# A channel layer as seven block products in place of eight, with its input kept per chunk in a ring

## The chip, the cores and the metric

The kernel runs on one core of one Trainium2 chip. The metric is the device time in microseconds (us) of one execution. Times are medians of several executions, beside executions of the kernel before on the same chip. "Granted clock" is the share of TensorE's full clock that the profile records. SBUF and PSUM are the core's two on-chip memories: in this program the inputs, weights and hidden values lie in SBUF, and the matmuls write PSUM. A relu is a maximum with 0. The engines are TensorE (PE; PEld is its weight load), VectorE (DVE), ScalarE (ACT), GpSimd (POOL) and SyncE (SP, which issues DMAs).

## The reference

For each of 8 batches of 3008 tokens x 256 features, the reference takes the real part of a 2-D Fourier transform, mixes the tokens, and applies a two-layer channel network with a residual:

```
X = np.fft.fft(np.fft.fft(x, axis=1), axis=2).real
h = np.maximum(X.transpose(0, 2, 1) @ w_tok1, 0.0) @ w_tok2
u = X + h.transpose(0, 2, 1)
h2 = np.maximum(u @ w_ch1, 0.0) @ w_ch2     # w_ch1 256 x 1536, w_ch2 1536 x 256
return u + h2
```

The change concerns the last product, `max(...) @ w_ch2`: per batch 3008 tokens x 1536 hidden units x 256 features.

## The kernel before

Tokens go in 48 chunks of 512 (six a batch). Each chunk is worked off in four quarters ("subs"). A quarter holds a quarter of this chunk's first layer (`mm1`, 6 matmuls of 512 columns), a quarter of the previous chunk's second layer (`mm2`, 12 matmuls of 256 columns), and between them pieces of the next batch's front (transform and token mixing). GpSimd "folds" the input of the batch after that: sums and differences of mirrored tokens and features.

```python
def mm1(b, c, c1, cts):                       # first layer + relu
    ...
        if ct % 3 < 2:
            nc.scalar.activation(out=c1[:, ct, 0:n], in_=pc[:, 0:n], func=AFT.Relu)
        else:
            ts(c1[:, ct, 0:n], pc[:, 0:n], 0.0, AT.max)           # VectorE
def mm2(b, c, c1, ks, box):                   # second layer, 128 tokens
    ...
    for ct in range(NCT if n else 0):         # NCT = 12 blocks of 128 hidden units
        nc.tensor.matmul(po[0:n, o:o + D], lhsT=c1[:, ct, ks * P:ks * P + n],
                         rhs=wc2[:, ct, :], start=(ct == 0), stop=(ct == NCT - 1))
    ...                                       # residual: VectorE, reads PSUM
def fold(b, engs):                            # engs: GpSimd for b >= 1
    for s, (t0, t1) in enumerate(((13, 17), (9, 13), (5, 9), (1, 5))):
        eng.tensor_tensor(out=xd[:, t, :], in0=xp[:, t, :], in1=rv, op=AT.subtract)
        eng.tensor_tensor(out=xp[:, t, :], in0=xp[:, t, :], in1=rv, op=AT.add)
        ...                                   # the same over mirrored features -> eo
        yield
```

## Time and profile before

The first executions took 630.45 us (630.44 to 632.22).

| engine | busy us | share of the span |
|---|---|---|
| PE | 608.3 | 97% |
| VectorE | 353.8 | 56% |
| ScalarE | 318.6 | 51% |
| GpSimd | 244.5 | 39% |

The page of the kernel before: the busy row, and the chain that ended last (the work, followed back from the last instruction) by engine.

```profile
PE 608.3 (97%) x4810; PEld 420.9 (67%) x4810; DVE 353.8 (56%) x809; ACT 318.6 (51%) x682; POOL 244.5 (39%) x234
...
PE 95%; ACT 2%; DVE 1%; issue 0%; DVEq 0%; POOL 0%; POOLq 0%
```

The waits of PE in the kernel before (who waited for whom: us in total, times, longest). The first line is the start-up; after it PE hardly waits.

```profile
PE pt L255 <- ACT tp L239: 11.7, 1, 11.7
PE po L598 <- DVE osb L615: 1.3, 2, 0.6
```

The chain of the kernel before in order of time (start us, us, what). Twelve second-layer matmuls of 256 columns take 1.31 us; 24 token-layer matmuls of 127 and 130 columns, each with its own weights, take 1.36 us.

```profile
366.51 1.36 PE pt L478 x24
...
369.19 1.31 PE po L598 x12
```

One line of the fold in the kernel before, on GpSimd and (in the start-up) on VectorE: count, then duration min/median/max in ns. On GpSimd it is 3.1 times as long, and its 28 durations differ by 17 ns at most: nothing disturbs it.

```profile
L413 POOL TENSOR_TENSOR xd<-xp,xm x28: 2110/2118/2127, 39.0 to 436.0; 94x1024 f16<-94x1024 f16 x28
...
L413 DVE TENSOR_TENSOR xd<-xp,xm x4: 675/678/678, 11.6 to 18.6; 94x1024 f16<-94x1024 f16 x4
```

So PE is the bound, and its time is the sum of what it streams.

### The profile page before, as it was taken

The page shows a single profiled execution, that of the slowest core. Times are in us where ns is not written, and L with a number is a line of the kernel's source. Part 1 is how long each engine was busy: PE and PEld are TensorE (multiplying, and loading weights), DVE is VectorE, ACT ScalarE, POOL GpSimd, SP SyncE. Part 2 cuts the span into 40 slices and gives each one's busy share as a digit, 9 for nine tenths or more (in the row PEclk, how much of TensorE's full clock was granted, in tenths as well). Part 3 has the DMA queues.
Part 4 walks back from the last instruction along what each step waited for, and adds up shares of the span by engine and source line. Part 5 has one row for each costly group of instructions (what it writes and reads, how often), then busy time and mean ns, then how long its engine had stood idle before and what let it go on. Part 6 is the DMA issues. An engine that isn't in the chain of part 4 may idle for free.

```text
span 628.7 us, 11983 instructions
## 1 busy us (share of the span) xinstructions
PE 608.3 (97%) x4810; PEld 420.9 (67%) x4810; DVE 353.8 (56%) x809; ACT 318.6 (51%) x682; POOL 244.5 (39%) x234
## 2 busy tenths in 40 slices
PE   2899999999999999999999999999999999999996
PEld 1766677667666766667666676667766676666664
DVE  8865455665654556455664557545565456544442
ACT  8875554644436453464435554374534654334441
POOL 8559698595033940369130880059200000000000
PEclk9999999999999999999999999999999999999999
DMA  9993835636315274333924258143223422335232
GB/s 143 212 182 100 157 66 96 134 68 133 72 34 110 60 145 61 82 63 63 168 58 68 66 100 139 35 93 68 52 51 76 77 52 54 80 68 85 60 84 67
DMA packets 86583, 56.28 MB, mean 90 GB/s; under 512 B 54864, under 2 KB 83472, under 8 KB 85776
## 3 DMA queue, kind: packets, MB, share of 16 engines
q1 hardware_dynamic: 78048, 37.84, 30.7%
q0 software_dynamic: 8256, 17.49, 16.2%
q8 instruction: 37, 0.61, 0.4%
q14 instruction: 18, 0.15, 0.1%
q10 hardware_dynamic: 224, 0.20, 0.1%
HBM read 34.98 MB, written 24.64 MB: 95 GB/s over the span
## 4 chain that ended last, share of the span: by engine, by line
PE 95%; ACT 2%; DVE 1%; issue 0%; DVEq 0%; POOL 0%; POOLq 0%
PE po L598 39%; PE pc L577 39%; PE pu L544 7%; PE pt L478 3%; PE pz L435 2%; PE pw L462 1%; PE pw L463 1%; PE py L509 1%; PE pq L509 1%; PE filler L273 1%; ACT tt L280 0%; PE ph L383 0%; PE ph L385 0%; PE pz L451 0%; ACT vq L308 0%
## 5 line engine op out<-in xcount | busy, mean ns | idle before, releaser
L580 ACT ACTIVATE c<-pc 128x512 f16<-128x512 f32 (+1 forms) x384 | 204.7, 586 | 164.6 <-PE pc L577 130.1
L598 PE MATMUL po<-wc,c 128*128 128x256 f16 x2256 | 276.8, 273 | 1.3 <-DVE osb L615 1.3
L598 PEld LDWEIGHTS <-c 128*128 128x128 f16 x2256 | 217.3, 98 | 49.6 <-issue 3.6
L87 DVE TENSOR_SCALAR c<-pc 128x512 f16<-128x512 f32 (+1 forms) x192 | 130.4, 679 | 125.7 <-PE pc L577 114.1
L577 PE MATMUL pc<-ut,wc1p 128*128 128x512 f16 x576 | 140.0, 379 | 0.0
L577 PE MATMUL pc<-ut,wc1m 128*128 128x512 f16 (+1 forms) x576 | 134.9, 371 | 0.0
L615 DVE TENSOR_TENSOR osb<-po,rt 128x258 f32<-128x258 f32 (+4 forms) x246 | 75.2, 356 | 50.4 <-PE po L598 47.7
L577 PEld LDWEIGHTS <-wc1m 128*128 128x128 f16 x576 | 54.8, 98 | 53.8
L577 PEld LDWEIGHTS <-wc1p 128*128 128x128 f16 x576 | 52.7, 98 | 48.3 <-issue 1.2
L552 DVE TENSOR_TENSOR ut<-pu,yt 128x512 f16<-128x512 f32 (+1 forms) x96 | 64.2, 670 | 20.1 <-PE pu L544 20.1
L413 POOL TENSOR_TENSOR xd<-xp,xm 94x1024 f16<-94x1024 f16 x28 | 59.3, 2118 | 14.4 <-DMA xm<-in_x_dram,ix 14.4
L635 POOL COPY ch<-c 128x768 f16<-128x768 f16 x4 | 3.3, 822 | 150.9 <-DVE c L87 150.9
L414 POOL TENSOR_TENSOR xp<-xp,xm 94x1024 f16<-94x1024 f16 x28 | 59.3, 2118 | 2.2
L418 POOL TENSOR_TENSOR eo<-xp 94x512 f16<-94x512 f16 (+1 forms) x28 | 33.9, 1211 | 59.0 <-PE pz L451 57.8
L637 POOL COPY c<-ch 128x768 f16<-128x768 f16 x4 | 3.3, 822 | 125.3 <-PE po L598 125.3
L280 ACT ACTIVATE w<-pw 128x127 f16<-128x127 f32 x96 | 26.1, 279 | 49.9 <-PE pw L463 49.9
L280 ACT ACTIVATE z<-pz 128x480 f16<-128x480 f32 (+1 forms) x60 | 38.9, 664 | 24.1 <-PE pz L435 18.6
L544 PE MATMUL pu<-w2p,uu 128*128 128x512 f16 (+1 forms) x168 | 50.0, 380 | 0.0
L516 DVE TENSOR_TENSOR yt<-py,qs 128x512 f16<-128x512 f32 x48 | 30.9, 686 | 27.5 <-PE pc L577 17.8
L465 DVE SCALAR_TENSOR_TENSOR w<-alt,pw 128x131 f16<-128x131 f16 x96 | 33.1, 350 | 18.3 <-ACT w L280 18.3
L422 POOL TENSOR_TENSOR eo<-xd 94x508 f16<-94x508 f16 (+1 forms) x28 | 33.7, 1203 | 0.0
L512 ACT ACTIVATE qs<-pq 128x512 f32<-128x512 f32 x24 | 14.4, 600 | 25.8 <-PE pq L509 18.0
(149 smaller groups left out, 402.2 us busy)
## 6 DMA issues: line engine op xcount, KB each, us to landing
out_dram<-osb SPq DMA_DIRECT2D x83, 256.0 KB, 3.5
xp<-in_x_dram POOLq DMA_DIRECT2D x16, 272.0 KB, 5.5
out_dram<-osb SPq DMA_DIRECT2D x11, 192.0 KB, 3.2
xp<-in_x_dram POOLq DMA_DIRECT2D x16, 127.5 KB, 6.0
rt<-ut SPq DMA_TRANSPOSE x96, 3.5
w2s<-in_moe_w_tok_dram POOLq DMA_DIRECT2D x1, 1504.0 KB, 17.5
w1p<-in_moe_w_tok_dram POOLq DMA_DIRECT2D x2, 384.0 KB, 8.8
wc<-in_moe_w_ch_dram POOLq DMA_DIRECT2D x1, 768.0 KB, 14.9
```

Of the source, the lines that this page charges most:

```text
L87: eng.tensor_scalar(out=out_, in0=in_, scalar1=s1, scalar2=None, op0=op0)
L280: nc.scalar.activation(out=out_, in_=in_, func=AFT.Copy)
L413: eng.tensor_tensor(out=xd[:, t, :], in0=xp[:, t, :], in1=rv, op=AT.subtract)
L414: eng.tensor_tensor(out=xp[:, t, :], in0=xp[:, t, :], in1=rv, op=AT.add)
L418: eng.tensor_tensor(out=eo[:, t, 1:129], in0=xp[:, t, 1:129], in1=xp[:, t, 255:127:-1], op=AT.add)
L422: eng.tensor_tensor(out=eo[:, t, 129:256], in0=xd[:, t, 1:128], in1=xd[:, t, 255:128:-1], op=AT.subtract)
L544: nc.tensor.matmul(pu[:, 0:n], lhsT=uu[:, th, int(minus), h, :], rhs=w2_cols(b, c)[:, th], start=(th == 0), stop=(th == 1))
L552: nc.vector.tensor_tensor(out=ut[:, h, f0:f0 + n].rearrange("p (a b) -> p a b", b=64), in0=pu[:, 0:n].rearrange("p (b a) -> p a b", b=64), ...
L577: nc.tensor.matmul(pc[:, 0:n], lhsT=wc[:, h, ct * P:(ct + 1) * P], rhs=ut[:, h, f0:f0 + n], start=(h == 0), stop=(h == 1))
L580: nc.scalar.activation(out=c1[:, ct, 0:n], in_=pc[:, 0:n], func=AFT.Relu)
L598: nc.tensor.matmul(po[0:n, o:o + D], lhsT=c1[:, ct, ks * P:ks * P + n], rhs=wc2[:, ct, :], start=(ct == 0), stop=(ct == NCT - 1))
L615: nc.vector.tensor_tensor(out=osb[r, ks_, j], in0=src[r, k0:k1, j], in1=rt[r, ks_, p], op=AT.add)
```

## The change

A Strassen (Winograd) split of each chunk's second layer: tokens, hidden units and features are each halved, and seven products of blocks take the place of eight. PE streams 84 matmuls of 128 columns a chunk in place of 48 of 256 (10752 columns for 12288). In exchange VectorE forms four sums of hidden blocks and seven sums of products a chunk, and four sums of weight blocks once. To make room, all relus go to ScalarE, the residual goes from VectorE to GpSimd, the folds are cut into finer pieces, and u is kept per chunk in a ring of four tiles. Six of the 48 chunks keep the old form ("plain").

```diff
+    def weight_sums():                        # once, batch 0, after quarter 5
+        tt(out=t1, in0=b12, in1=b11, op=AT.subtract)
+        copy(1, wst[:, 0], t1)                # VectorE cast
+        tt(out=t2, in0=b22, in1=t1, op=AT.subtract)
+        copy(1, wst[:, 1], t2)
+        tt(out=wst[:, 2], in0=b22, in1=b12, op=AT.subtract)
+        tt(out=wst[:, 3], in0=b21, in1=t2, op=AT.subtract)
...
+    def plain(b, c):
+        return (b, c) == (0, 0) or c + 1 == NCH and (b % 2 == 0 or b + 1 == BB)
...
-            if ct % 3 < 2:
+            if i % 3 < 2 or (b, c) != (0, 0):            # all relus on ScalarE
...
+    def hidden_sums(c1, sb, k, which):        # VectorE, 1536 elements each, both inputs in SBUF
+        sums = ((sb[:, 0, k], a21, a22, AT.add),
+                (sb[:, 1, k], sb[:, 0, k], a11, AT.subtract),
+                (a21, a11, a21, AT.subtract),
+                (sb[:, 2, k], a12, sb[:, 1, k], AT.subtract))
...
+    def mm2_sums(b, c, c1, s, box):
+        if s == 0:
+            product(0, lambda k: c1[:, k], 0, lambda k: wc2[:, k, wa])
+            product(1, lambda k: c1[:, HC + k], 0, lambda k: wc2[:, HC + k, wa])
+            ...
+        elif s == 1:                          # needs sums 0 and 1, and wst
+            product(0, lambda k: sb[:, 1, k], 0, lambda k: wst[:, 1, k])
+            product(1, lambda k: sb[:, 0, k], 0, lambda k: wst[:, 0, k])
+            ...
+        elif s == 2:                          # needs sums 2 and 3
+            product(0, lambda k: c1[:, k], 1, lambda k: wst[:, 2, k])
+            product(1, lambda k: sb[:, 2, k], 0, lambda k: wc2[:, HC + k, wb])
+            ...
+            residual(nc.gpsimd, osb[:, 0:2], osb[:, 0:2], rt[:, 0:2], minus)
+        else:
+            product(0, lambda k: c1[:, HC + k], 1, lambda k: wst[:, 3, k])
+            ...
...
+    fold_at = [15, 10]                        # folds: 8 quarters from here, 2 pieces each, GpSimd
```

More of the change, by code (lines that the diff above doesn't have):

```diff
@@ L220, in load_wc2 @@
         gdma(wc2[:], dram(wc2_t, 0, [[D, P], [P * D, NCT], [1, D]]))
+    HC = NCT // 2
+    wst = const.tile([P, 4, HC, P], FP16, tag="wst")
+    def weight_sums():
+        b11, b12, b21, b22 = (wc2[:, HC * j:HC * j + HC, P * k:P * k + P]
+                              for j in range(2) for k in range(2))
+        t1, t2 = (work.tile([P, 4, D], FP32, tag="osb", name="wsum", bufs=3)[:]
+                  .rearrange("p k d -> p (k d)")[:, 0:HC * P]
+                  .rearrange("p (k d) -> p k d", k=HC) for _ in range(2))
+        tt = nc.vector.tensor_tensor
+        tt(out=t1, in0=b12, in1=b11, op=AT.subtract)
[4 more added lines that the diff above has]
+        tt(out=wst[:, 3], in0=b21, in1=t2, op=AT.subtract)
     def swap_wc1(h):
@@ L405, in fold @@
         xp, xm = x_tiles.pop(b)
-        xd = perb.tile([KR, NR, D], FP16, tag="xd", name="xd")
         eo = perb.tile([KR, NR, D], FP16, tag="eo", name="eo")
@@ L411, in fold @@
             t = slice(t0, t1)
+            lo = 0 if t0 == 1 else t0
+            xd = perb.tile([KR, 5, D], FP16, tag="xd", name="xd")
+            td = slice(t0 - lo, t1 - lo)
             rv = xm[0:KR, 16 - t0:(16 - t1 if t1 < 17 else None):-1, :]
-            eng.tensor_tensor(out=xd[:, t, :], in0=xp[:, t, :], in1=rv, op=AT.subtract)
+            eng.tensor_tensor(out=xd[:, td, :], in0=xp[:, t, :], in1=rv, op=AT.subtract)
+            yield
             eng.tensor_tensor(out=xp[:, t, :], in0=xp[:, t, :], in1=rv, op=AT.add)
+            yield
             if t0 == 1:
-                t = slice(0, t1)
+                t = td = slice(0, t1)
                 eng.tensor_copy(out=xd[:, 0, :], in_=xp[:, 0, :])
@@ L421, in fold @@
                               in1=xp[:, t, 0:1], op=AT.add)
-            eng.tensor_tensor(out=eo[:, t, 129:256], in0=xd[:, t, 1:128],
-                              in1=xd[:, t, 255:128:-1], op=AT.subtract)
+            yield
+            eng.tensor_tensor(out=eo[:, t, 129:256], in0=xd[:, td, 1:128],
+                              in1=xd[:, td, 255:128:-1], op=AT.subtract)
             yield
@@ L524, in front @@
         yield
-        ut = perb.tile([P, 2, NCH * CW], FP16, tag="ut", name="ut", bufs=2)
-        if b % 2:
-            nc.vector.tensor_copy(out=ut[:, :, S:NCH * CW],
-                                  in_=state[b - 1]["ut"][:, :, S - 64:S])
-        else:
-            nc.vector.memset(ut[:, :, S:NCH * CW], 0.0)
-        st["ut"] = ut
+        uts = st["ut"] = []
         for c in range(NCH):
@@ L539, in front @@
             n = min(CW, S - f0)
+            ut = perb.tile([P, 2, CW], FP16, tag="ut", name="ut", bufs=4)
+            if n < CW and b % 2:
+                nc.vector.tensor_copy(out=ut[:, :, n:CW], in_=state[b - 1]["tail"][:])
+            elif n < CW:
+                nc.vector.memset(ut[:, :, n:CW], 0.0)
+            uts.append(ut)
             for h in range(2):
@@ L552, in front @@
                 nc.vector.tensor_tensor(
-                    out=ut[:, h, f0:f0 + n].rearrange("p (a b) -> p a b", b=64),
+                    out=ut[:, h, 0:n].rearrange("p (a b) -> p a b", b=64),
                     in0=pu[:, 0:n].rearrange("p (b a) -> p a b", b=64),
                     in1=y.rearrange("p (a b) -> p a b", b=64), op=AT.add)
+                if h and n < CW and b % 2 == 0:
+                    st["tail"] = perb.tile([P, 2, 64], FP16, tag="tail", name="tail")
+                    nc.vector.tensor_copy(out=st["tail"][:], in_=ut[:, :, n - 64:n])
                 yield
@@ L565, in turn_u @@
                 out=rt[:, :, h * P:(h + 1) * P],
-                in_=state[b]["ut"][:, h, CW * c:CW * c + CW])
+                in_=state[b]["ut"][c][:, h, :])
         return rt
+    CTS = [0, 6, 1, 7, 2, 8, 3, 9, 4, 10, 5, 11]
+    def plain(b, c):
+        return (b, c) == (0, 0) or c + 1 == NCH and (b % 2 == 0 or b + 1 == BB)
     def mm1(b, c, c1, cts):
-        ut = state[b]["ut"]
-        f0 = CW * c
-        n = min(CW, S - f0)
+        ut = state[b]["ut"][c]
+        n = min(CW, S - CW * c)
         wc = wc1[c >= 3]
-        for ct in cts:
+        for i in cts:
+            ct = CTS[i]
             pc = ps_mm("pc")
@@ L577, in mm1 @@
                 nc.tensor.matmul(pc[:, 0:n], lhsT=wc[:, h, ct * P:(ct + 1) * P],
-                                 rhs=ut[:, h, f0:f0 + n], start=(h == 0), stop=(h == 1))
-            if ct % 3 < 2:
+                                 rhs=ut[:, h, 0:n], start=(h == 0), stop=(h == 1))
+            if i % 3 < 2 or (b, c) != (0, 0):
                 nc.scalar.activation(out=c1[:, ct, 0:n], in_=pc[:, 0:n], func=AFT.Relu)
@@ L582, in mm1 @@
                 ts(c1[:, ct, 0:n], pc[:, 0:n], 0.0, AT.max)
+    def hidden_sums(c1, sb, k, which):
+        hi = slice(HC + k.start, HC + k.stop)
+        a11, a21 = c1[:, k, 0:D], c1[:, k, D:CW]
+        a12, a22 = c1[:, hi, 0:D], c1[:, hi, D:CW]
+        sums = ((sb[:, 0, k], a21, a22, AT.add),
+                (sb[:, 1, k], sb[:, 0, k], a11, AT.subtract),
+                (a21, a11, a21, AT.subtract),
+                (sb[:, 2, k], a12, sb[:, 1, k], AT.subtract))
+        for i in which:
+            o, x, y, op = sums[i]
+            nc.vector.tensor_tensor(out=o, in0=x, in1=y, op=op)
@@ new lines, in residual, with product, add @@
+    def residual(eng, osb, src, rt, minus):
+        adds = [(slice(minus, P + 1 - minus), slice(minus, P + 1 - minus)),
+                (slice(P + 1, D), slice(D - 1, P, -1))]
+        if minus:
+            adds.append((slice(0, P + 1, P), slice(P, None, -P)))
+        for j, p in adds:
+            eng.tensor_tensor(out=osb[:, :, j], in0=src[:, :, j], in1=rt[:, :, p],
+                              op=AT.add)
+    def mm2_sums(b, c, c1, s, box):
+        minus = int(c >= 3)
+        if s == 0:
+            box["osb"] = work.tile([P, 4, D], FP32, tag="osb", name="osb", bufs=3)
+            box["m"] = work.tile([P, 3, 2, P], FP32, tag="m", name="m")
+        osb, rt, sb, m = (box[i] for i in ("osb", "rt", "sb", "m"))
+        po = ps_out("po")
+        half = po[:].rearrange("p (i t d) -> p i t d", i=2, t=2)
+        wa, wb = slice(0, P), slice(P, D)
+        def product(i, a, hi, w):
+            for t in range(2):
+                f = D * hi + P * t
+                for k in range(HC):
+                    nc.tensor.matmul(half[:, i, t], lhsT=a(k)[:, f:f + P], rhs=w(k),
+                                     start=(k == 0), stop=(k == HC - 1))
+        def add(o, i, y):
+            nc.vector.tensor_tensor(out=o, in0=half[:, i], in1=y, op=AT.add)
+        if s == 0:
+            product(0, lambda k: c1[:, k], 0, lambda k: wc2[:, k, wa])
+            product(1, lambda k: c1[:, HC + k], 0, lambda k: wc2[:, HC + k, wa])
+            nc.scalar.activation(out=m[:, 0], in_=half[:, 0], func=AFT.Copy)
+            add(osb[:, 0:2, wa], 1, m[:, 0])
+        elif s == 1:
+            product(0, lambda k: sb[:, 1, k], 0, lambda k: wst[:, 1, k])
+            product(1, lambda k: sb[:, 0, k], 0, lambda k: wst[:, 0, k])
+            add(m[:, 1], 0, m[:, 0])
+            add(m[:, 2], 1, m[:, 1])
+        elif s == 2:
+            product(0, lambda k: c1[:, k], 1, lambda k: wst[:, 2, k])
+            product(1, lambda k: sb[:, 2, k], 0, lambda k: wc2[:, HC + k, wb])
+            add(m[:, 1], 0, m[:, 1])
+            add(osb[:, 2:4, wb], 0, m[:, 2])
+            add(osb[:, 0:2, wb], 1, m[:, 2])
+            residual(nc.gpsimd, osb[:, 0:2], osb[:, 0:2], rt[:, 0:2], minus)
+        else:
+            product(0, lambda k: c1[:, HC + k], 1, lambda k: wst[:, 3, k])
+            add(osb[:, 2:4, wa], 0, m[:, 1])
+            residual(nc.gpsimd, osb[:, 2:4], osb[:, 2:4], rt[:, 2:4], minus)
+        if s == 3:
+            for i in range(2):
+                nk = 3 if c + 1 == NCH and i else 4
+                nc.sync.dma_start(
+                    out=dram(out_t, (b * S + 8 * c + i) * D,
+                             [[NQ * D, 64], [2 * D, nk], [1, D]]),
+                    in_=osb[64 * i:64 * i + 64, 0:nk, :])
+            if c + 1 == NCH:
+                nc.sync.dma_start(
+                    out=dram(out_t, ((b - 1) * S + NQ - 1) * D, [[NQ * D, 64], [1, D]]),
+                    in_=osb[64:P, 3, :])
@@ L584, in mm2 @@
     def mm2(b, c, c1, ks, box):
+        if not plain(b, c):
+            return mm2_sums(b, c, c1, ks, box)
         last = c + 1 == NCH
-        n = P
-        if last and ks == 3 and b % 2 == 0:
-            n = 64 if b + 1 == BB else 0
-        minus = int(c >= 3)
+        final = last and b + 1 == BB
+        n = 0 if last and ks == 3 and b % 2 == 0 else P
         if ks == 0:
@@ L592, in mm2 @@
         osb, rt = box["osb"], box["rt"]
-        if ks % 2 == 0:
+        if final:
+            box["po"] = (ps_out, ps_mm)[ks % 2]("po")
+        elif ks % 2 == 0:
             box["po"] = ps_out("po")
@@ L600, in mm2 @@
                              start=(ct == 0), stop=(ct == NCT - 1))
-        final = last and b + 1 == BB
         if ks % 2 == 1 or final:
@@ L609, in mm2 @@
                 ks_ = slice(ks - ks % 2 + k0, ks - ks % 2 + k1)
-                adds = [(slice(minus, P + 1 - minus), slice(minus, P + 1 - minus)),
-                        (slice(P + 1, D), slice(D - 1, P, -1))]
-                if minus:
-                    adds.append((slice(0, P + 1, P), slice(P, None, -P)))
-                for j, p in adds:
-                    nc.vector.tensor_tensor(out=osb[r, ks_, j], in0=src[r, k0:k1, j],
-                                            in1=rt[r, ks_, p], op=AT.add)
+                residual(nc.vector, osb[r, ks_], src[r, k0:k1], rt[r, ks_], int(c >= 3))
         first = 2 if final and ks == 3 else 0
@@ L634, in pair @@
             state["ch"] = work.tile([P, NCT, 64], FP16, tag="ch", name="ch")
-            nc.gpsimd.tensor_copy(out=state["ch"][:], in_=c1[:, :, CW - 128:CW - 64])
+            nc.vector.tensor_copy(out=state["ch"][:], in_=c1[:, :, CW - 128:CW - 64])
         elif b % 2:
-            nc.gpsimd.tensor_copy(out=c1[:, :, CW - 64:CW], in_=state["ch"][:])
+            nc.vector.tensor_copy(out=c1[:, :, CW - 64:CW], in_=state["ch"][:])
     def take(g, n):
@@ L647 @@
     pieces = fold(0, [nc.vector] * 4)
-    take(pieces, 1)
+    take(pieces, 4)
     table_d()
-    take(pieces, 3)
+    take(pieces, 12)
     turn(tq, tts_q, 4)
@@ L673 @@
     if BB > 1:
-        take(fold(1, [nc.gpsimd] * 4), 4)
+        take(fold(1, [nc.gpsimd] * 4), 16)
     if BB > 2:
@@ L678 @@
     work = ctx.enter_context(tc.tile_pool(name="work", bufs=1))
-    plan = [[0] * 10 + [2] * 10 + [2, 1, 2, 1],
-            [2] * 10 + [1, 1, 1, 2, 1, 2, 1, 2, 1, 1, 1, 1, 1, 1]]
+    plan = [[0] * 10 + [2] * 14,
+            [1] * 13 + [0] + [2, 1] * 5]
+    fold_at = [15, 10]
+    own_plan = [[2, 1, 1, 1, 1, 1, 1, 0, 1, 1, 0, 0, 1, 1] + [0] * 10,
+                [1, 1, 1, 0, 0, 1, 1, 0, 1, 1, 0, 0, 1, 1] + [0] * 10]
     prev = None
@@ L687 @@
         nxt = front(b + 1) if b + 1 < BB else iter(())
-        done, folded = 0, False
+        folds = fold(b + 2, [nc.gpsimd] * 4) if b + 2 < BB else None
         for c in range(NCH):
@@ L691 @@
             box = {"rt": turned_u.pop((b, c))}
+            if not plain(b, c):
+                box["sb"] = work.tile([P, 3, HC, D], FP16, tag="sb", name="sb", bufs=2)
+            if c + 1 == NCH and b % 2:
+                pair(b, c1)
             for s in range(4):
@@ L695 @@
                 mm1(b, c, c1, range(3 * s, 3 * s + 3))
-                if sub < 12:
-                    take(own, 1)
+                sums = prev is not None and not plain(*prev[0:2])
+                if s == 0 and sums:
+                    hidden_sums(prev[2], pbox["sb"], slice(0, HC), (0, 1))
+                take(own, own_plan[b > 0][sub])
                 take(nxt, n // 2)
+                if s == 1 and sums:
+                    hidden_sums(prev[2], pbox["sb"], slice(0, HC), (2, 3))
                 if prev is not None:
                     mm2(*prev, s, pbox)
-                if b == 0 and sub < 8:
-                    align_w2(sub)
+                if b == 0 and sub < 16 and sub % 2:
+                    align_w2(sub // 2)
                 take(nxt, n - n // 2)
-                done += n
                 if s == 2 and c + 1 < NCH:
@@ L708 @@
                     turned_u[b + 1, 0] = turn_u(b + 1, 0)
+                if b == 0 and sub == 5:
+                    weight_sums()
                 if b == 0 and sub == 3:
@@ L711 @@
                         swap_wc1(h)
-                if done >= 8 and not folded:
-                    folded = True
-                    if b + 2 < BB:
-                        take(fold(b + 2, [nc.gpsimd] * 4), 4)
-                    if b + 3 < BB:
+                if folds is not None and sub >= fold_at[b > 0]:
+                    take(folds, 2)
+                    if sub == fold_at[b > 0] + 7 and b + 3 < BB:
                         x_tiles[b + 3] = load_x(b + 3)
-            if c + 1 == NCH:
+            if c + 1 == NCH and b % 2 == 0:
                 pair(b, c1)
```

## The prediction

> **What bounds the kernel now.** The tensor engine (PE). The page's busy row gives PE 97% of 628.7 us, VectorE (DVE) 56%, ScalarE (ACT) 51%, GpSimd (POOL) 39%. The chain that ended last is PE for 95%: second layer (po) 39%, first layer (pc) 39%. In the waits, PE waits under 2 us for others after the start-up. The granted clock is 1.0 throughout. So the time is the sum of PE's streaming.
>
> **What PE saves.** In the chain in order of time, 12 second-layer matmuls of 256 columns take 1.31 us (109 ns each); a full chunk has 48: 5.24 us. The change gives 7 products x 2 token blocks x 6 = 84 matmuls of 128 columns, each with its own weight load. Same-sized matmuls with their own weights are in this trace: the token layer (pt, 127 and 130 columns) does 24 in 1.36 us, 56.7 ns each. The Trainium skill ("TensorE: Matmul & The Clock Gate", Back-to-back issue gap) gives about 81 ns for a sustained stream of 128-column pairs; this trace disagrees, and the trace decides. 84 x 56.1 ns (56.7 scaled to 128 columns) = 4.71 us, so 0.53 us less per chunk. 42 of 48 chunks use it (six stay plain): 22.4 us, all on the critical path. Floor about 608 us.
>
> **What is added and moved** (per changed chunk of about 11.9 us):
> - ACT takes all 12 relus (4 more x 0.59 us) and one PSUM copy (about 0.4 us): busy 319 to about 445 us, 73%. Not limiting.
> - DVE loses 4 relus (0.68 us each) and the residual adds (about 1.6 us), gains four hidden sums of 1536 fp16 elements (the fold's 1024-element form takes 0.68 us, so about 0.94 us each: 3.8 us) and seven PSUM adds of 256 columns (0.41 us each, as the residual's: 2.9 us). Busy 354 to about 455-470 us, 75% on average, 85-90% in the second half of a batch, where the next batch's front also needs it.
> - POOL gains the residual from SBUF: at the fold's about 2 ns an element plus 0.2, about 3 us a chunk; 245 to about 365 us.
>
> **What eats the gain.** The hidden sums are new dependences in front of PE: products 3 to 6 wait for DVE, with about 2 us slack at the second quarter of a chunk and 0.5 to 1 us at the third. Until now no steady-state DVE instruction had two SBUF inputs; the sums do, beside POOL's 2.1 us folds. The Trainium skill ("SBUF — State Buffer", Who interferes with whom) states that such a DVE instruction and a GpSimd instruction that reads SBUF exclude each other for a whole instruction. No steady stretch of this trace shows it. In the fold windows (about 30 us in six batches) each sum could wait 0-2 us, more than the slack. I estimate 3-12 us of PE idle in all, most likely 5.
>
> **Prediction:** 613 us, 80% range 606 to 630. Faster by over 2%: 0.62; within 2%: 0.31; slower: 0.07.
>
> **What would show each step.** Second-layer groups of 12 matmuls of 128 columns take about 0.67 us in the chain. PE busy falls by 20-23 us. Hidden sums average 0.95 us without and over 1.3 us with contention; the fold's 1024-element form on POOL rises above its steady 2.12 us (2.11 to 2.13 before). PE's waits name DVE hidden sums (second or third quarter), mostly while POOL folds; fewer name ACT relus holding the three pc buffers. ACT about 73% busy, DVE about 75%.
>
> **What would make it wrong.** Weight loads holding the 128-column matmuls near 80 ns (then slower by over 5%); DVE and POOL excluding each other so strongly that DVE becomes the bound in fold windows (near 630); POOL falling so late that folds or residual buffers stall the front; or slack ample everywhere (608).

## The result, and the profile after

The changed kernel took 649.73 us (648.1 to 650.91, 4 runs) beside 631.34 (630.44 to 632.32, 4 runs). The ratio is 1.0295, with a 95% interval of 1.0272 to 1.0318. A ratio here is the mean time of one kernel's runs over that of the other's of the same rounds, so not quite the ratio of the medians. Executions over 1.5% slower than the fastest of the same kernel are left out of the means. The result is correct, but the kernel became slower by 3%, and the prediction (613 us, 606 to 630) was wrong.

The page of the changed kernel: busy row, the granted TensorE clock in 40 slices (tenths), and the chain by engine. PE's share fell to 92%, and the clock has a hole early on and two small dents. The chain follows PE for only 22% of the span, because it breaks off at a wait that it cannot follow.

```profile
PE 595.6 (92%) x6322; PEld 422.7 (65%) x6322; DVE 507.2 (78%) x895; ACT 417.8 (64%) x912; POOL 430.4 (66%) x432
...
PEclk9999699999999999899999999989999999999999
...
PE 22%; DVE 1%; issue 0%; DVEq 0%
```

The chain of the changed kernel in order of time: 24 matmuls of 128 columns in 1.34 us.

```profile
507.21 1.34 PE po L648 x24
```

The windows view of batch 6 in the kernel before (481.96 to 556.39 us) and then in the changed one (505.31 to 576.44), where no fold runs: us of the stretch, then busy us and instructions of PE, PEld, DVE, ACT, POOL, then clock, DMA share, GB/s. PE is busy throughout in both, and the batch is 3.30 us shorter: 0.55 us for each of its six changed chunks. This is the gain that was intended.

```profile
481.96:556.39 74.43, 74.43 (x590) 51.46 (x588) 41.36 (x92) 36.60 (x80) 0.76 (x1) 1.00 0.32 65
```

```profile
505.31:576.44 71.13, 71.13 (x805) 51.63 (x804) 57.60 (x106) 49.31 (x110) 25.40 (x38) 1.00 0.37 75
```

The waits of PE in the changed kernel. `sb` and `c` at L623 are the hidden sums.

```profile
PE po L648 <- DVE sb L623: 27.5, 17, 8.1
...
PE pu L565 <- DVE ut L573: 2.7, 5, 0.5
...
PE po L648 <- DVE c L623: 1.2, 5, 0.3
```

The ledger, worked out from the two traces from the first layer's first matmul on: PE's idle time (gaps over 0.15 us), and lost clock, which is the sum of (1 - granted share) x time while PE works. Where the clock was low while PE waited anyhow, the time stands under idle alone.

| | span | PE idle | lost clock | rest |
|---|---|---|---|---|
| before | 628.7 | 1.3 | 0.0 | 627.4 |
| after | 648.3 | 32.2 | 6.2 | 610.0 |

The rest fell by 17.4 us where 22.4 were predicted. The full saving is there when PE hardly waits: in run d_write_only below, with three waits, the rest is 605.0, which is 22.4 less than before. By an estimate, most of what is missing here belongs to the waits too: a 128-column matmul is recorded with 0.22 us while the next one of a stream starts 0.056 us later, so each of the 29 waits (two before) costs about 0.16 us more, which the records show as busy. The two losses that ate the gain came to 38 us in the ledger, where the prediction had 3 to 12.

**First loss: the weight sums.** The timeline of VectorE in the changed kernel (start us, us, instructions). Six instructions hold VectorE for 13.4 us in a row.

```profile
53.26 2.43 DVE L232 TENSOR_TENSOR wsum<-wc 128x768 f32<-128x768 f16 x1
55.73 2.36 DVE L295 CAST wst<-wsum 128x768 f16<-128x768 f32 x1
58.01 1.90 DVE L234 TENSOR_TENSOR wsum<-wc,wsum 128x768 f32<-128x768 f16 x1
59.94 1.54 DVE L295 CAST wst<-wsum 128x768 f16<-128x768 f32 x1
61.41 2.47 DVE L236 TENSOR_TENSOR wst<-wc 128x768 f16<-128x768 f16 x1
63.81 2.86 DVE L237 TENSOR_TENSOR wst<-wc,wsum 128x768 f16<-128x768 f16 x1
```

The same stretch on PE: the first product that reads a hidden sum waits 8.12 us, and its 24 matmuls then span 2.74 us in place of about 1.5 (these records run to the last matmul's end), because the clock was granted at half for 10.24 us from 66.7 us on. Of these, 4.7 us lie inside the wait and cost nothing more; the other 5.6 us cost 2.8. Together 8.1 us idle and 2.8 us of lost clock.

```profile
71.38 2.74 PE L648 MATMUL po<-wst,sb 128*128 128x128 f16 x24 [8.12 <-DVE sb L623]
```

**Second loss: the hidden sums beside the folds.** The timeline of GpSimd in the changed kernel in a fold stretch, then that of VectorE. Each is a list of single instructions.

```profile
169.45 2.12 POOL L434 TENSOR_TENSOR xp<-xp,xm 94x1024 f16<-94x1024 f16 x1
171.65 1.75 POOL L439 TENSOR_TENSOR eo<-xp 94x512 f16<-94x512 f16 x1
173.36 0.22 POOL L441 TENSOR_TENSOR eo<-xp 94x4 f16<-94x4 f16 x1
```

```profile
169.88 2.52 DVE L623 TENSOR_TENSOR sb<-c 128x1536 f16<-128x1536 f16 x1
172.43 1.94 DVE L623 TENSOR_TENSOR sb<-sb,c 128x1536 f16<-128x1536 f16 x1
```

A hidden sum takes 0.95 us when it is alone. The first one here starts at 169.88, but GpSimd's fold ends at 171.57; 171.57 plus 0.95 is 172.52, and the sum ends at 172.40, so the two agree to 0.12 us. The next fold starts at 171.65 and takes 1.75 us in place of its steady 1.15: it waited for the sum. The second sum waits for that fold and the small instruction behind it in turn. The records count such a wait as busy time. PE pays for it:

```profile
174.43 1.51 PE L648 MATMUL po<-wst,sb 128*128 128x128 f16 x24 [1.01 <-DVE sb L623]
```

Over the whole run the 168 hidden sums took 225.0 us, a mean of 1.34, where 168 x 0.95 is 160. Twenty of them took over 2.3 us. Each of the 72 that took over 1.1 us ended 0.8 to 1.0 us after the end of a GpSimd instruction. PE's 24 us of other idle time lies in batches 0 to 5, the ones with folds. In batches 6 and 7 PE does not wait at all.

### The profile page after: what moved, and what is told of

It reads as the page before. It is cut to its first block, busy times and chain, and to the rows that moved or that the text cites. A ratio compares the mean times of both kernels' runs of the same rounds, so it can differ in the third digit from the quotient of the medians.

```text
span 648.3 us, 15738 instructions
## 1 busy us (share of the span) xinstructions
PE 595.6 (92%) x6322; PEld 422.7 (65%) x6322; DVE 507.2 (78%) x895; ACT 417.8 (64%) x912; POOL 430.4 (66%) x432
## 5 line engine op out<-in xcount | busy, mean ns | idle before, releaser
L609 ACT ACTIVATE c<-pc 128x512 f16<-128x512 f32 (+1 forms) x572 | 295.7, 591 | 102.2 <-PE pc L606 91.4
L631 POOL TENSOR_TENSOR osb<-osb,rt 128x258 f32<-128x258 f32 (+2 forms) x206 | 154.1, 775 | 186.0 <-DVE osb L652 101.6
L648 PEld LDWEIGHTS <-c 128*128 128x128 f16 x2016 | 121.9, 98 | 22.2 <-DVE c L623 2.5
L648 PEld LDWEIGHTS <-sb 128*128 128x128 f16 x1512 | 89.3, 99 | 41.1 <-DVE sb L623 35.1
L652 DVE TENSOR_TENSOR osb<-po,m 128x256 f32<-128x256 f32 x168 | 66.6, 417 | 44.4 <-PE po L648 33.1
L648 PE MATMUL po<-wst,sb 128*128 128x128 f16 x1008 | 64.5, 221 | 17.2 <-DVE sb L623 17.2
L648 PE MATMUL po<-wst,c 128*128 128x128 f16 x1008 | 70.8, 220 | 1.2 <-DVE c L623 1.2
L623 DVE TENSOR_TENSOR sb<-sb,c 128x1536 f16<-128x1536 f16 x42 | 68.5, 1630 | 1.4
L648 PE MATMUL po<-wc,c 128*128 128x128 f16 x1008 | 63.1, 219 | 0.0
L623 DVE TENSOR_TENSOR sb<-c 128x1536 f16<-128x1536 f16 x42 | 56.8, 1352 | 7.2 <-ACT c L609 7.2
L623 DVE TENSOR_TENSOR sb<-c,sb 128x1536 f16<-128x1536 f16 x42 | 58.4, 1389 | 0.0
```

Source lines behind the costliest of these rows:

```text
L623: nc.vector.tensor_tensor(out=o, in0=x, in1=y, op=op)
L631: eng.tensor_tensor(out=osb[:, :, j], in0=src[:, :, j], in1=rt[:, :, p], op=AT.add)
L648: nc.tensor.matmul(half[:, i, t], lhsT=a(k)[:, f:f + P], rhs=w(k), start=(k == 0), stop=(k == HC - 1))
L652: nc.vector.tensor_tensor(out=o, in0=half[:, i], in1=y, op=AT.add)
```

## The experiments

Theories. **Lock:** a VectorE instruction with two SBUF inputs and a GpSimd instruction that reads SBUF exclude each other, so the hidden sums arrive late. The Trainium skill ("SBUF — State Buffer", Who interferes with whom) states this exclusion. **Load:** VectorE has simply too much to do in front of the sums. **Moves:** the relus on ScalarE, the ring, the finer folds or the new order cost time by themselves.

### a_moves_alone: everything but the seven products

```diff
     def plain(b, c):
-        return (b, c) == (0, 0) or c + 1 == NCH and (b % 2 == 0 or b + 1 == BB)
+        return True                           # and no weight_sums()
```

> All 48 chunks use the old second layer of 8 block products; no hidden sums, no weight sums; every other move stays (relus on ScalarE, ring of u, finer folds, new order of the front). If the loss comes from what the seven-product form adds (the lock theory and the VectorE load theory alike), PE stays the bound and the time is that of the kernel before, 631 us within 4. If the moves themselves cost (relus all on ScalarE holding the three pc buffers, the ring of four u tiles, late folds), the time is over 637 us and PE waits name ScalarE relus, u or eo.

Measured: 629.84 us beside 630.44, ratio 0.9986 (0.9965 to 1.0007), correct. After the start PE idles 0.0 us. The moves cost nothing; that theory falls. (This run keeps the residual on VectorE; b, c and d have it on GpSimd.)

### b_no_hidden_sums: the matmuls without the sums

```diff
-            nc.vector.tensor_tensor(out=o, in0=x, in1=y, op=op)      # the four hidden sums
...
-            product(0, lambda k: sb[:, 1, k], 0, lambda k: wst[:, 1, k])
+            product(0, lambda k: c1[:, k], 0, lambda k: wst[:, 1, k])  # and so for the other two
```

> Wrong result on purpose: the four hidden sums a chunk are left out, and the same matmuls read the hidden values themselves. PE then waits for VectorE only at the weight sums. If the seven products cost PE what was predicted (56.1 ns a matmul), the floor of about 608 us plus the start-up stall of the weight sums (8.1 us of idle and about 5 us of lower clock in the changed kernel; less here if the sums' own 3.4 us behind them are gone) gives 615 to 622 us. If 128-column matmuls were slower than that in this place, or the seven PSUM additions held PE, the time stays over 630 us.

Measured: 613.64 us (607.33 to 614.40), ratio 0.9691, wrong result; a little under the expected 615 to 622. PE idles 4.0 us, all behind the weight sums. Without idle time and lost clock the profiled span is 605.5 (627.4 before). So the seven products give what they should, and neither 128-column matmuls nor the seven PSUM additions hold PE. The exclusion shows from the other side as well: without the sums the two main fold groups on GpSimd take 2.13 and 2.15 us on average (2.33 and 2.44 in the changed kernel), and GpSimd is busy 354.1 us for 430.4.

### c_no_folds and d_write_only: GpSimd without folds, and GpSimd that only writes

```diff
-        folds = fold(b + 2, [nc.gpsimd] * 4) if b + 2 < BB else None
+        folds = iter(()) if b + 2 < BB else None          # c: batch 1's folded input again
...
+        folds = stand_in(b + 2) if b + 2 < BB else None   # d: instead of c's line
+    def stand_in(b):
+        for s in range(4):
+            for n in (2, 2, 1, 1):
+                for _ in range(n):
+                    nc.gpsimd.memset(xd[:, 0:5, :], 0.0)
+                yield
```

> Wrong result on purpose: the folds of batches 2 to 7 on GpSimd are left out (the folded input of batch 1 is used again); VectorE executes exactly the instructions of the changed kernel. Lock theory: outside the first batch the hidden sums fall from a mean of 1.34 us to about 1.05 us (only the residual additions on GpSimd are left to meet), PE waits for them vanish after batch 0, and the time falls by about 25 us to 620-626 us (the weight-sum stall of about 13 us stays). VectorE load theory: VectorE has as much to do as before, so the waits and the time stay near 645-650 us.

> Wrong result on purpose: as the run without folds, but GpSimd instead fills the same scratch tile with zeros, six instructions of 1280 fp16 elements in place of each quarter of a fold, so that it stays busy writing SBUF and reads none. If the exclusion is one of SBUF reads, the hidden sums and the time are those of the run without folds within 3 us. If any GpSimd work beside VectorE (writes, or the mere activity) stretches the sums, the sums stay well over 1.1 us in the windows where GpSimd is busy and the time lies above that of the run without folds by 5 us or more.

Measured: c 616.11 us (ratio 0.9756), d 616.86 us (ratio 0.9780), both wrong results. VectorE's instruction list is that of the changed kernel in both; the time is 33 us lower. After batch 0 PE waits for no sum in c, and in d once, for 0.3 us (a sum that met the residual additions, which still read SBUF on GpSimd). The sums themselves, in the changed kernel first, then in c, then in d (ns min/median/max):

```profile
L623 DVE TENSOR_TENSOR sb<-c,sb x42: 944/952/2874, 73.6 to 633.7; 128x1536 f16<-128x1536 f16 x42
```

```profile
L623 DVE TENSOR_TENSOR sb<-c,sb x42: 945/951/1425, 73.5 to 600.5; 128x1536 f16<-128x1536 f16 x42
```

```profile
L633 DVE TENSOR_TENSOR sb<-c,sb x42: 943/953/1465, 71.4 to 598.1; 128x1536 f16<-128x1536 f16 x42
```

In d GpSimd is busy 393.6 us (64%; 66% in the changed kernel). Its timeline, then VectorE's, in one such stretch: the sums take 0.94 to 0.96 us beside it.

```profile
174.76 9.79 POOL L456 MEMSET xd<- 94x1280 f16 x8
```

```profile
176.06 0.94 DVE L633 TENSOR_TENSOR sb<-c 128x1536 f16<-128x1536 f16 x1
177.03 0.96 DVE L633 TENSOR_TENSOR sb<-sb,c 128x1536 f16<-128x1536 f16 x1
```

So what excludes is GpSimd's reading of SBUF, not its activity (one writing instruction, MEMSET, was tried): the lock theory holds, and the load theory falls for the steady part. The fall was larger than expected (616 for 620 to 626); the weight-sum stall was smaller here, 6.0 us of idle and 2.3 of lost clock in c (8.1 and 2.8 in the changed kernel), and the two later dents of the clock, 1.7 us each, are gone too.

### e_weights: the weight sums out of the way

```diff
-        return (b, c) == (0, 0) or c + 1 == NCH and ...
+        return b == 0 and c < 3 or c + 1 == NCH and ...
...
-        copy(1, wst[:, 0], t1)
+        copy(0, wst[:, 0], t1)                # ScalarE; a yield after each sum
...
-                if b == 0 and sub == 5:
-                    weight_sums()
+                if b == 0 and sub == 5:
+                    weights = weight_sums()
+                if b == 0 and 5 <= sub < 9:
+                    take(weights, 1)
```

> Correct result. The sums of the second layer's weights are spread: one addition a quarter over four quarters, the two conversions on ScalarE, and the first batch's chunks 1 and 2 stay plain so that nothing waits for them. The trace of the changed kernel puts 8.1 us of PE idle and 5.1 us of lower clock on them; two chunks lose 0.53 us of gain each. So 649.7 - 13.2 + 1.1 = 637.6 us, within 4. If the stall were only moved (VectorE short of time there anyhow), the time stays over 645 us.

Measured: 643.36 us, ratio 1.0173, correct. Batch 0 fell from 83.1 to 75.9 us and the wait of 8.1 us is gone, but the gain was 6.4 us, about half of what was expected. The forecast had added 5.1 us of lower clock to the 8.1 us of idle, but 2.3 of them lie inside the wait (see the first loss). Later folds met sums in batch 0 (2.4 us of idle in its last chunk), and the clock dropped at two places, near 109 and 187 us, where it had not. PE's idle time is 24.6 us, lost clock 6.7. The rest is 611.3, which is 1.3 more than in the changed kernel; the two plain chunks explain 1.1.

### f_spread, g_spread_half, k_dense_half: the folds spread, and cut in half

All three start from e_weights. f spreads the same folds over 17 quarters in place of 8; g does so with half the length of each instruction; k halves the length without spreading.

```diff
-                if folds is not None and sub >= fold_at[b > 0]:
-                    take(folds, 2)
+                a, z = fold_at[b > 0], fold_to[b > 0]     # f, g: 7 to 23; k: 10 to 17 (b > 0)
+                if folds is not None and a <= sub <= z:
+                    due = [N * (i - a) // (z - a + 1) for i in (sub, sub + 1)]
+                    take(folds, due[1] - due[0])          # N: 16 in f, 32 in g and k
...
+            for a in range(t0, t1, g):                    # fold: g = 4 tokens in f, 2 in g and k
```

> Correct result. As e_weights, and the GpSimd folds of batches 3 to 7 are spread over 17 quarters of a chunk in place of 8, the same instructions of 1024 elements. Lock theory: a sum that meets a fold waits as long as before (single sums up to 2.9 us remain), but the pauses between folds make it rarer: half to two thirds of the 24 us of waits in the fold windows remain, 626 to 634 us. Had the density of the folds been the whole trouble, it goes below 620 us.

> Correct result. As f_spread, with every fold instruction halved (512 elements in place of 1024, 256 in place of 512): GpSimd's busy time rises by its fixed cost of about 0.2 us an instruction, VectorE's work is untouched. Lock theory: no sum waits for more than about 1.2 us, so no sum takes over about 2.2 us, the slack of PE suffices nearly always, and the time falls to 612-620 us, under both kernels. VectorE load theory: no change against f_spread.

> Correct result. As e_weights (folds on GpSimd in the same quarters of a chunk, not spread), with every fold instruction halved. It parts the two things that g_spread_half changed. If the length of one GpSimd instruction is what makes a sum late (a sum waits for the rest of one instruction), the longest sums fall from 2.9 to about 2.0 us, PE's idle time after the start from 24.6 us to under 12 us, and the time from 643 to 625-634 us. If only the total of GpSimd's reading counts, no gain: 640 us or more, since halving adds to it.

| run | us | ratio to before | sums over 2.3 us | PE idle | lost clock | chunks with PE idle over 0.2 us |
|---|---|---|---|---|---|---|
| e_weights | 643.36 | 1.0173 | 20 | 24.6 | 6.7 | 15 |
| f_spread | 662.55 | 1.0479 | 22 | 38.1 | 6.7 | 21 |
| g_spread_half | 640.35 | 1.0163 | 7 | 20.6 | 1.7 | 17 |
| k_dense_half | 632.46 | 1.0020 | 7 | 16.3 | 0.0 | 14 |

A difference counts from 2% on: f is slower than before and k is the same; e and g are unclear (1.0141 to 1.0204 and 1.0116 to 1.0209).

Spreading was expected to help and cost 19 us: as many sums took over 2.3 us as before, and waits stood in more chunks. PE waited in 21 chunks, and for other things too (2.6 us for ScalarE relus, 1.9 us that the profile puts on nothing). Why the collisions did not become rarer was not settled. Halving the instructions helped in both pairs (f to g by 22 us, e to k by 11 us; of these, 5.0 and 6.7 us are lost clock that did not recur) although it adds to GpSimd's work, so the length of one GpSimd instruction matters; but neither g nor k beat the kernel before. The forecast for g (612 to 620 us) failed. That for k held in the time (625 to 634) but not in its steps: PE idles 16.3 us for under 12, and the longest sum took 2.86 us for about 2.0. In g the longest sum took 3.86 us. Its VectorE timeline, then its GpSimd timeline:

```profile
390.28 3.86 DVE L629 TENSOR_TENSOR sb<-c 128x1536 f16<-128x1536 f16 x1
```

```profile
390.14 0.67 POOL L448 TENSOR_TENSOR eo<-xp 94x256 f16<-94x256 f16 x1
390.77 1.30 POOL L637 TENSOR_TENSOR osb<-osb,rt 128x258 f32<-128x258 f32 x2
392.03 0.66 POOL L451 TENSOR_TENSOR eo<-xd 94x254 f16<-94x254 f16 x1
392.65 0.67 POOL L448 TENSOR_TENSOR eo<-xp 94x256 f16<-94x256 f16 x1
```

The sum ended at 394.14; less 0.95 it began in earnest near 393.2, after five GpSimd instructions. These short ones follow without a pause, each recorded as starting about 0.04 us before the last one ends. VectorE did not get its turn after the first of them. The long ones in the changed kernel leave 0.08 us between, and there it did. A missing pause alone does not decide: over the traces of all nine runs with hidden sums, a waiting sum came next in all 103 places where GpSimd paused for about 0.08 us, and in 396 of 448 where it did not pause (a sum that took over 1.1 us is counted at the GpSimd instruction whose end lies nearest to the sum's end less 0.95). What decides in the other 52 stays open; no run tested it.

### h_fold_vector: more work for VectorE

```diff
# against f_spread
-        folds = fold(b + 2, [nc.gpsimd] * 4, 4) if b + 2 < BB else None
+        folds = fold(b + 2, [nc.vector] * 4, 4) if b + 2 < BB else None
```

> Correct result. As f_spread, but the folds of batches 2 to 7 run on VectorE (0.68 us for 1024 elements): it gets about 9.5 us more of its own work a batch, and GpSimd keeps only the residual additions. Lock theory: waits inside the sums nearly vanish (mean of a sum under 1.15 us); VectorE's busy share is that of e_weights within 5%, in spite of the added work, and the time falls to 612-626 us. VectorE load theory: more work on VectorE makes it slower than e_weights, 645 us or more.

Measured: 616.36 us, ratio 0.9758 (0.9736 to 0.9780), correct. One word against f_spread takes away 46 us. VectorE was given all folds of batches 2 to 7, and its busy time is 494.5 us, for 489.5 in e_weights and 506.0 in f_spread: the added work is what the waits inside its instructions used to take. No sum takes over 1.42 us, and PE idles 5.4 us. This is the strongest evidence against the load theory.

### i_best: the same, tuned

```diff
# against h_fold_vector
-        return b == 0 and c < 3 or c + 1 == NCH and ...
+        return b == 0 or c + 1 == NCH and ...
...
-        folds = fold(b + 2, [nc.vector] * 4, 4) ...
+        folds = fold(b + 2, [nc.vector if b else nc.gpsimd] * 4, 4) ...
...
+    fold_at, fold_to = [15, 6], [23, 21]
```

> Correct result. As h_fold_vector, with batch 0 all plain (two chunks fewer with seven products, 1.1 us lost, but no sums beside the start-up's folds, and the fold of batch 2 stays on GpSimd where no sum meets it), and the VectorE folds moved two quarters of a chunk ahead. Batch 0 falls from 73.2 to about 71.3 us (what it takes with the moves alone), batch 1 from 71.9 to about 71: 613 us, within 2, clearly under the 631 of the kernel before.

Measured: 610.57 us (610.29 to 611.88, 5 runs), ratio 0.9671 (0.9658 to 0.9684), correct: faster than both kernels, and somewhat under the expected 613. The page's busy row of this kernel, and below it the two largest waits of PE, both in the start-up:

```profile
PE 588.5 (97%) x6178; PEld 421.2 (69%) x6178; DVE 472.7 (78%) x974; ACT 417.9 (69%) x910; POOL 264.3 (43%) x307
```

```profile
PE pt L276 <- ACT tp L260: 11.7, 1, 11.7
PE pt L276 <- ACT tt L286: 1.2, 1, 1.2
```

After the start PE idles 0.3 us. The span without idle time and lost clock is 608.2 us, 19.2 less than before, with 38 chunks of seven products in place of 42. The change is worth its arithmetic once nothing that reads SBUF through GpSimd stands beside the sums for long.

## Why the prediction was wrong

- **What bounds the kernel, and what PE saves: right.** 24 matmuls of 128 columns take 1.34 us, 55.8 ns each (predicted 56.1). Without idle time and lost clock PE needs 22.4 us less in d_write_only (predicted 22.4), and 17.4 less in the changed kernel, with its many waits. The 81 ns that the Trainium skill gives for this ("TensorE: Matmul & The Clock Gate", Back-to-back issue gap) does not hold here, as the trace of before had shown.
- **ScalarE: right in kind.** It is not limiting: 64% (predicted 73%).
- **VectorE and GpSimd busy: too low.** VectorE 507 us for 455 to 470, GpSimd 430 for 365. VectorE's excess is the waiting inside its instructions: 225.0 - 160 = 65 us in the hidden sums alone; without it, it would be 442. On GpSimd the two main fold groups rose from 2.12 to a mean of 2.33 and 2.44 us; without the sums (b) GpSimd is busy 354 us.
- **The step that failed: "I estimate 3-12 us of PE idle in all, most likely 5."** It was 32.2 us, and 6.2 us of lost clock on top, which the sum did not contain. The mechanism was the one named: VectorE's sums and GpSimd's folds exclude each other, and the waits lie in fold stretches; runs c, d and h show it. The size was wrong by the prediction's own numbers: it allowed each sum 0 to 2 us of waiting against 0.5 to 2 us of slack, for about 30 us (two to three chunks; it became about 40, 156.5 to 196.6 us in batch 1) in each of six batches, and then did not multiply. Two chained sums each wait, and both stand in front of PE; 24 us of idle in the fold stretches of six batches is 4 us a batch.
- **The weight sums were left out.** The prediction did not cost them at all. Six VectorE instructions of about 2.3 us, in a row, beside GpSimd's start-up folds, cost 8.1 us of idle and 2.8 us of clock (e_weights won back 6.4 us net, less than this sum).
- **"VectorE and GpSimd excluding each other so strongly ... (near 630)"** was listed as what could go wrong, and was itself too small by 20 us.
- **Folds or residuals too late, relus holding the pc buffers:** these did not happen to any extent; no wait of PE in the changed kernel names them.

## What to carry to other kernels

When a change puts VectorE instructions with two SBUF inputs in front of the bounding engine, look first at what GpSimd does at that time: an instruction of 2 us that reads SBUF can delay a sum of 0.95 us to 2.9 us, and the record shows it as busy time, so compare durations with the same form alone before reading a busy share as load. Moving GpSimd's elementwise work to VectorE can then make VectorE no busier, since the work replaces waits (494 us busy for 506, and 46 us faster here). Multiply a possible wait by the number of places where it exceeds the slack, and cost one-time set-up work in the queue where it lands.

## What the Trainium skill lacked or had wrong

- "TensorE: Matmul & The Clock Gate", Back-to-back issue gap: about 81 ns for a sustained matmul of 128 columns with its own weight load. The runs show 24 in 1.34 us, 55.8 ns each.
- The same page, HAM oscillation: it tells to avoid idle gaps of PE over about 3.4 us (its next section says that frequent short idle times can lower the clock too, without a length). Here the clock was granted at half for 3.41 us after much shorter ones: in the changed kernel at 271.5 us, after gaps of 1.29 and 0.54 us within 3 us, and in g_spread_half at 128.7 us, after a single gap of 1.94 us. Not every such gap did it.
- "SBUF — State Buffer", Who interferes with whom: the exclusion is confirmed, also that a GpSimd instruction that only writes does not exclude a sum (0.94 to 0.96 us beside fills). The page says that whoever issues first gets the ports; it does not say who comes next when one engine waits and the other has more to do. Mostly the waiting sum came next, as after the GpSimd instruction of 2.12 us, but in 52 places a further GpSimd instruction went first, in one case until five had passed (a sum of 3.86 us).
- "GPSIMD Engine Reference", Engine selection: about twice as slow as VectorE for two-input operations. For fp16 with 1024 elements it was 3.1 times (2.12 us for 0.68).
